# A gated recurrence with a convolution feed-forward on one core: state and head products of a tile's first chunk joined, the last convolution tap joined to the value product, a shorter gate chain, a new order of all steps

## The chip, the cores and the metric

One core of a Trainium2 chip. The time is the device time of one execution in microseconds, median over runs; lower is better.

## What is computed

For each of 4 batches and 8 heads (768 steps, head size 40) a recurrence runs over time, and its gated output (320 features a token) goes through a gated feed-forward. Cut to what matters:

```python
# per step t, for each batch and head
m_new = max(f_gate[t] + m, i_gate[t])
f_stab = exp(f_gate[t] + m - m_new);  i_stab = exp(i_gate[t] - m_new);  m = m_new
C = f_stab * C + i_stab * outer(v[t], k[t]);   n = f_stab * n + i_stab * k[t]
y[t] = sigmoid(o_gate[t]) * (C @ q[t]) / max(abs(n @ q[t]), 1)
# x = y with heads side by side: (4, 768, 320)
gate = sigmoid(sum_k conv_w[k] * x[t - 4 + k])        # 5 taps, per feature
out  = (gate * (x @ w_val)) @ w_out
```

## The kernel before

The recurrence is computed in chunks of 64 steps. Time is cut into 6 tiles of 128 tokens (`j`), each tile into two chunks (`p` = 0, 1), and for each tile and batch (`b`) there is a unit `u = 4j + b` and a group `g = 2u + p`: 48 groups of 8 heads. For one group:

- `args` (L582) makes the exponents of the decay matrix by one matmul from two packed tables, `la` and `ra`, that come from the gates; `expo` (L586) is their exponential on ScalarE, `scores` (L599) the products of q and k (fp16 pieces), `probs` (L604) their product on VectorE, into `pk[:, h, 0:64]`.
- `keyw` (L612, VectorE or GpSimd) puts the weighted unit keys beside it, into `pk[:, h, 64:104]`.
- `heads` (L639) multiplies `pk[:, h, 0:64]` (64 columns of weights) with the values and the incoming state `vc`: 8 products in float32, each of which the engine runs as two records, 16 in all. The first chunk's output stands in partitions 0 to 63 of a bank, the second's in 64 to 127 of the same bank. `state` (L622) multiplies `pk[:, h, 64:104]` (40 columns) with the same values, 16 records into another bank, and `stout` (L631) copies the new state out.

`norm` (L654, L656, L658: three small VectorE operations on the bank), `rsm` (L662) and `gate` (L665) finish a unit of x. `xtr` (L687) transposes x; `xhc`, `xcc`, `x3c`, `xlo`, `xeh`, `xel` split it into a rounded float32r part and a rest. Features 0 to 255 are convolved on GpSimd and VectorE (`cv0` L723, `cv` L729). The last 64 features stand twice, as high and low part, in the 128 partitions of `x3`, and are convolved on TensorE: `cv3` (L750), 5 taps with diagonal weights `cdh` and 5 with `cdl`. `g3c` copies that out, `sigm` (L761) is the sigmoid, `val` (L771) the value product, for three blocks of columns (`m` = 0, 1 with 128 columns, `m` = 2 with 64), 8 matmuls each; `zmul`, `zhi`, `zlo` and `outp` (L794, 8 matmuls per batch) make the output. The inputs of a tile are scaled, cut into fp16 pieces (`hi` L540, `lo` L549) and transposed by TensorE (`trp`, first tiles) or DMA (`trd`, L561).

At the start the gates go through a chain, `gates` (steps 0 to 11, once for tile 0 and once for the rest): a scan for the running maximum, differences, a clamp, a running sum, and a split into three bf16 pieces (`gsp`), which DMAs carry through DRAM into `la` and `ra`.

Nothing is scheduled at run time. `PLAN` is a string of steps with their arguments, `=V`, `=A`, `=P`, `=S` naming the engine or queue, `#n` the PSUM bank (8 banks); steps are issued in that order, so each engine's queue is its own part of the string. All engines wait for each other by semaphores where data or buffers ask for it; two `pk` and three `dm` buffers alternate over the groups.

Of the kernel before, what the change touches and what calls it, by code (L numbers as in the profile page):

```python
# [24 lines left out]
ldc.3=S zrst0.1=V scs.0.0.2.0.1.1=V gates.0.6=V hi.0.0.0=A hi.0.0.1=P raj.4=V ldc.2=S ldq.1.3=S mx.0.3.1=A ovc.0.0=P
scs.0.0.2.0.1.3=V gates.0.3=P gates.1.4=V ldo.1=S raj.2=A fsel.1=P mx.0.2.1=A ldk.1.2.4=S gates.0.7=V fsel.2=P
idk0.2=V gates.0.8=A raj.3=P raj.5=A cpk.0.1.0=V ovc.0.1=P zvc.0=V ctl=P wcv.5.5=A mx.0.2.0=A mx.1.3.0=A lo.0.0.0=V
gates.1.5=P mx.0.3.0=A scs.0.0.2.2.3.0=V idk1.1=A lo.0.0.1=V ovc.1.0=P wcv.5.0=V gates.0.9=V ftl.1=P scs.0.0.2.1.2.0=V
gates.0.10=V scs.0.0.2.1.2.1=V scs.0.0.2.3.4.0=V gates.0.11=P hi.0.1.1=A id16c=P soa.0.2=S hi.0.1.0=P soa.0.1=A
trp.0.0.1#0 lo.0.1.1=V trp.0.0.0#1 ldk.1.0.2=S idk1.0=A lo.0.1.0=V soa.0.3=S mx.1.1.0=A raj.1=V trp.0.1.0#2  # L30
scs.0.0.2.3.4.1=V trc.0.0.1=V hi.0.3.0=V ldo.0=S wcv.5.1=V lo.0.3.0=V wld.0.0=S sigo.1=A gates.1.3=V trp.0.3.0#3
zcmp.1.0=V wcv.5.2=V laj=V mx.1.3.1=A trp.0.1.1#4 scs.0.0.2.2.3.1=V scs.0.0.2.0.1.2=V scs.0.0.2.1.2.2=V hi.0.2.1=A
gates.1.6=V mx.1.1.1=A hi.0.3.1=A raj.0=V soa.0.0=S wcv.5.3=V sog.0=A gates.1.7=V mx.1.2.1=A cla.1=S wcv.5.4=V
gates.1.8=V mx.1.2.0=A hi.0.2.0=V gates.1.9=P trc.0.0.0=A trc.0.1.0=V trc.0.1.1=V mx.1.0.1=A lo.0.2.0=V mx.1.0.0=A
scores.3#5 sia.0.0=S sig_.0=S lo.0.3.1=V sigo.0=A trp.0.2.0#6 scs.1.0.1.0.4.0=V zxc=V wcv.0.0=V lo.0.2.1=V sia.0.1=S
trc.0.3.0=A scs.1.1.2.0.4.0=V cpk.0.0.1=S trp.0.3.1#7 scs.0.0.2.3.4.2=V wcv.0.1=V ldv.0.0=S scs.0.0.2.2.3.3=V
scores.1#0 scs.0.0.2.1.2.3=V scs.0.0.2.3.4.3=V zcmp.1.1=V ldq.2.1=S wcv.0.2=V gates.1.10=V scores.0#2
scs.1.0.1.0.4.1=V wcv.0.3=V args.0#1 trp.0.2.1#4 selg=V expo.0=A ldv.0.1=S wcv.5.6=V wcv.0.4=V args.3#3 trc.0.2.0=A
scs.1.1.2.0.4.1=V zcmp.0.0=V scores.2#1 trc.0.2.1=V cpk.0.1.1=S hi.1.1.1=P sct0=V hi.1.0.0=A scores.4#4 keyw.0=V
probs.0=V args.1#6 hi.1.1.0=A lo.1.0.0=V heads.0#2 expo.1=A lo.1.1.0=V ldk.2.0.2=S trc.0.3.1=A state.0#6 probs.1=V  # L40
ldq.2.3=S expo.3=A keyw.1=V scores.5#0 gates.1.11=V trp.1.0.0#7 stout.0=A args.2#3 chh=A scs.0.0.2.2.3.2=V args.4#6
cdd.0.1=P expo.2=A heads.1#2 ldq.2.2=S soa.1.3=A probs.2=V state.1#3 ldq.2.0=S scs.1.1.2.0.4.2=V heads.2#1 chl=V
wld.1.1=S norm.0.0=V stout.1=A probs.3=V cdd.1.3=P zx3=P wcv.0.5=A soa.1.1=S keyw.2=V hi.1.2.0=A trp.1.1.0#3
norm.0.1=V sog.1=S norm.0.2=V state.2#5 expo.4=A rsm.0=V soa.1.2=S hi.1.0.1=A probs.4=V args.5#6 keyw.4=P soa.1.0=S
expo.5=A wcv.0.6=V heads.4#4 hi.1.3.0=P wld.1.0=S trc.1.0.0=V stout.2=A mx.2.2.0=A cla.0=S open_late=X keyw.3=V
args.6#6 ovc.1.1=P lo.1.3.0=V heads.3#1 mx.2.1.0=A lo.1.2.0=V mx.2.3.0=A state.4#5 smul.1=V gate.0=V trc.1.1.0=A
state.3#7 lo.1.0.1=V probs.5=V sia.1.1=S whi.0.0=A trp.1.2.0#2 wld.2.1=S expo.6=A stout.3=V wlo.0.0=P trp.1.0.1#3
mx.2.0.0=A lo.1.1.1=V sig_.1=S keyw.5=P hi.1.2.1=A trc.1.2.0=V trp.1.1.1#0 wld.2.0=S mx.2.0.1=A scores.7#6 keyw.6=V
xeh.0=P hi.1.3.1=V sout.1#7 trp.1.3.0#2 stout.4=A xel.0=P wcv.1.0=V sia.1.0=S state.5#5 norm.1.0=V trc.1.3.0=A
scs.2.0.1.0.4.0=V trc.1.0.1=V ldk.2.2.4=S heads.5#4 wcv.1.1=V ldv.1.0=S wcv.1.5=A sctc.1=A scs.1.1.2.0.4.3=V args.7#3  # L50
norm.1.1=V lo.1.3.1=V scores.6#2 expo.7=A norm.1.2=V wcv.1.2=V state.6#7 mx.2.1.1=A probs.6=V keyw.7=P cpk.1.0.0=S
args.8#3 norm.2.0=V stout.6=A lo.1.2.1=V rsm.1=P scores.8#2 expo.8=A probs.7=V args.10#7 heads.6#3 zstk.0=P gate.1=V
cdd.1.4=P cpk.1.1.0=S zstk.1=P scs.2.0.1.0.4.1=V wcv.1.3=V mx.2.2.1=A ldq.3.3=S xtr.0#6 probs.8=V hi.2.0.0=A wcv.1.4=P
ldq.3.2=S state.7#1 smul.2=V xhc.0=A hi.2.1.0=P ldv.1.1=S lo.2.0.0=V heads.7#3 mx.2.3.1=A ldq.3.0=S expo.10=A
norm.2.1=V args.9#2 stout.7=V scores.9#7 xeh.1=V expo.9=A keyw.8=P stout.5=V args.11#1 trc.1.1.1=A norm.3.0=V
wcv.2.0=V trp.1.2.1#5 wcv.1.6=V state.8#2 norm.3.1=V xcc.0=A norm.2.2=V xel.1=V expo.11=A scs.2.1.2.0.4.0=V rsm.2=P
scs.2.1.2.0.4.1=V trp.1.3.1#0 ldq.3.1=S stout.8=A lo.2.1.0=V keyw.10=P xtr.1#1 cpk.1.0.1=S x3c.0=A sout.2#2 hi.2.1.1=A
sctc.2=V probs.9=V scores.10#6 trd.2.0.0=S hi.2.0.1=P args.13#2 trc.1.2.1=A gate.2=V heads.8#7 keyw.9=V ldk.3.0.2=S
lo.2.1.1=V state.10#4 xeh.2=V lo.2.0.1=V scores.11#5 stout.10=A xhc.1=V norm.3.2=V wcv.2.5=A heads.9#7 wcv.2.1=V
trd.2.0.1=S rsm.3=P trc.1.3.1=A probs.10=V state.9#4 cdd.1.0=P probs.11=V xcc.1=A heads.10#6 mx.3.2.0=A gate.3=V  # L60
hi.2.2.0=P trd.2.1.0=S mx.3.0.0=A whi.1.0=V heads.11#6 mx.3.3.0=A norm.4.0=V wcv.2.2=V keyw.11=V x3c.1=A cpk.1.1.1=S
expo.13=A args.12#0 norm.5.0=V args.14#5 xeh.3=V lo.2.2.0=V expo.12=A ldv.2.0=S scores.13#3 xel.3=P wcv.2.3=V
mx.3.1.0=A xtr.3#1 ldv.2.1=S norm.5.1=V cdd.0.0=A norm.5.2=V state.11#2 wlo.1.0=V expo.14=A rsm.5=P probs.13=V
hi.2.3.0=A scores.12#0 keyw.12=P gate.5=V xcc.3=A trd.2.1.1=S probs.12=V cdd.0.4=A xlo.0=P state.12#5 stout.11=A
# [867 lines left out]
```

## Time and profile before

| what | us |
|---|---|
| median of 3 runs (259.67 to 263.06) | 260.73 |
| the profiled execution, its own time | 261.67 |
| its span, first to last instruction | 259.8 |
| outside the span | 1.9 |

The durations below come from the profiled execution. The engines run beside each other, so their busy times do not add up to the span; which engine's work stands on the chain that ends last is shown by the chain of waits.

### The profile page before, as it was taken

Reading aid. Unit: us, or ns where it says so; the run is one execution under the profiler, and the core shown is the slowest. Engines: PE = TensorE matmul, PEld = TensorE weight load, DVE = VectorE, ACT = ScalarE, POOL = GpSimd, SP = SyncE. Lnnn points to the kernel's source line nnn. Section 1 sums busy time; section 2 is a strip of 40 time slices with the busy share of each in tenths; the row PEclk is TensorE's granted clock in tenths of the full one; section 3 lists DMA queues with packets and bytes.
Section 4 is the critical chain, followed back from the end, with each engine's and each line's share of the span. In section 5 each row is a group of like instructions: output and inputs, shape, how many; then the busy total and the mean of one; then the engine's idle time right before and its main releaser. Section 6 shows DMA issues by size and latency. Waiting matters only on the chain.

```text
span 259.8 us, 6790 instructions
## 1 busy us (share of the span) xinstructions
PE 218.0 (84%) x2539; PEld 184.8 (71%) x2539; DVE 220.1 (85%) x547; ACT 174.1 (67%) x381; POOL 107.1 (41%) x171
## 2 busy tenths in 40 slices
...
PEclk9999995569999959999999999999999999999999
DMA  8999699799669999979999999699860313001122
GB/s 132 176 169 185 151 144 202 162 174 187 124 96 154 195 209 212 204 116 185 192 159 178 183 193 162 108 176 201 143 112 0 48 46 95 1 28 50 50 103 101
DMA packets 130231, 35.77 MB, mean 138 GB/s; under 512 B 118310, under 2 KB 128086, under 8 KB 130198
## 3 DMA queue, kind: packets, MB, share of 16 engines
...
q8 instruction: 20, 0.33, 0.5%
q10 hardware_dynamic: 560, 0.16, 0.3%
q14 instruction: 13, 0.11, 0.1%
...
## 4 chain that ended last, share of the span: by engine, by line
PE 47%; DVE 22%; DMA 11%; ACT 6%; SPq 6%; issue 5%; POOL 1%; ACTq 0%; DVEq 0%; POOLq 0%
PE bank L639 12%; PE bank L794 8%; PE bank L771 7%; PE bank L622 6%; DVE sg L729 4%; DVE stk L549 4%; DMA tq<-stk 4%; DMA nat<-in_q_dram 4%; PE bank L599 4%; PE bank L582 3%; PE bank L750 3%; PE bank L566 3%; DMA nat<-in_k_dram 2%; PE bank L687 2%; DVE pk L604 2%
## 5 line engine op out<-in xcount | busy, mean ns | idle before, releaser
L639 PEld LDWEIGHTS bank<-vc,pk 104*64 104x64 f32 (+1 forms) x768 | 52.0, 149 | 11.5 <-issue 3.3
L639 PE MATMUL bank<-vc,pk 104*64 104x41 f32 (+1 forms) x768 | 57.1, 241 | 2.6 <-DVE stk L549 1.8
L604 DVE SCALAR_TENSOR_TENSOR pk<-bank,cmp,dm 128x512 f32<-128x512 f32 x48 | 35.5, 743 | 9.3 <-PE bank L599 3.1
L586 ACT ACTIVATE dm<-bank 128x512 f32<-128x512 f32 x48 | 28.4, 600 | 14.7 <-PE bank L582 12.2
L622 PE MATMUL bank<-vc,pk 128*40 128x41 f32 (+1 forms) x704 | 37.2, 212 | 0.9 <-ACT vc L631 0.5
L729 DVE SCALAR_TENSOR_TENSOR sg<-xc,cwt,sg 128x512 f32<-128x512 f32 (+1 forms) x56 | 37.3, 687 | 0.2
L599 PE MATMUL bank<-tq,tk 120*128 120x64 f16 x384 | 27.7, 241 | 11.0 <-DVE tk L570 5.9
L622 PEld LDWEIGHTS bank<-vc,pk 128*40 128x40 f32 (+1 forms) x704 | 32.5, 126 | 3.8 <-issue 2.1
L599 PEld LDWEIGHTS <-tk 120*128 120x128 f16 x384 | 22.5, 119 | 16.4 <-issue 6.7
L540 ACT ACTIVATE stk<-nat,scl 128x640 f16<-128x640 f32 x33 | 27.3, 829 | 6.3 <-PE bank L566 2.9
L566 PE MATMUL bank<-idh,stk 128*120 128x128 f16 x128 | 13.9, 287 | 20.5 <-POOL idh L342 19.1
L549 DVE SCALAR_TENSOR_TENSOR stk<-nat,scl,stk 128x320 f16<-128x320 f32 x48 | 27.4, 578 | 4.2 <-ACT stk L540 2.6
L612 POOL TENSOR_TENSOR pk<-kp,dm 104x320 f32<-104x320 f32 (+1 forms) x23 | 18.9, 827 | 28.8 <-ACT dm L586 12.5
L566 PEld LDWEIGHTS <-stk 128*120 128x120 f16 x128 | 12.7, 193 | 21.2 <-POOL vc L375 17.7
L494 ACT ACTIVATE junk<-nat 128x320 bf16<-128x320 f32 x48 | 22.5, 468 | 7.7 <-DMA nat<-in_k_dram 4.6
L631 ACT COPY vc<-bank 40x328 f32<-40x328 f32 x36 | 15.4, 426 | 16.1 <-PE bank L622 15.7
L662 POOL TENSOR_TENSOR rs<-sg,den 128x320 f32<-128x320 f32 x14 | 11.6, 831 | 28.7 <-DVE den L658 28.6
L582 PE MATMUL bank<-ra,la 120*128 120x512 bf16 x48 | 19.1, 424 | 1.7 <-ACT dm L586 1.6
L794 PE MATMUL bank<-woh,zh 128*128 128x320 f32 x72 | 19.6, 328 | 0.0
L794 PE MATMUL bank<-wol,zh 128*128 128x320 f32 x72 | 18.5, 310 | 0.0
L723 POOL TENSOR_SCALAR sg<-xc,cwt 128x512 f32<-128x512 f32 (+1 forms) x14 | 10.4, 746 | 13.0 <-DVE zl L786 11.1
L544 POOL TENSOR_SCALAR stk<-nat,scl 128x640 f16<-128x640 f32 x10 | 9.1, 912 | 15.5 <-DVE ob L798 6.6
...
## 6 DMA issues: line engine op xcount, KB each, us to landing
...
```

What stands on the lines that cost most here:

```text
L494: A.activation(junk, part(j, x, i), AF.Abs, accum_out=amx[j % 2][:, x, i : i + 1])
L540: A.activation(o, s, AF.Copy, scale=f)
L549: V.scalar_tensor_tensor(t[:, :, c : c + D], part(j, x, i), scl[j % 2][:, x, i : i + 1], t[:, :, 0:D], op0=ALU.mult, op1=ALU.subtract,)
L566: nc.tensor.transpose(t[0:K3, h], stk[(j * B + i) % NSTK][:, x, h, 0:K3], id16)
L582: nc.tensor.matmul(psd, la[:, p, j, b], ra[:, :, j], start=True, stop=True)
L586: A.activation(dms[g % NDM], late["psd", g], AF.Exp)
L599: nc.tensor.matmul(o, tk[h], tq[:, h], start=True, stop=True)
L604: V.scalar_tensor_tensor(pks[g % NPK][:, :, 0:L], late["pss", g], cmp_[j % 2][:, p, b : b + 1], dms[g % NDM], op0=ALU.mult, op1=ALU.mult,)
L622: nc.tensor.matmul(pc[n0 : n0 + D, h], pks[g % NPK][0:n, h, L:], vc[j % 2][0:n, p, b * H + h], start=True, stop=True)
L639: nc.tensor.matmul(ph[p * L : (p + 1) * L, h], pks[g % NPK][0:n, h, 0:L], vc[j % 2][0:n, p, b * H + h], start=True, stop=True,)
L729: V.scalar_tensor_tensor(o, xc[j % 2][:, c, b0:b1, t : t + P], cwt[:, c, t : t + 1], o, op0=ALU.mult, op1=ALU.add)
L794: nc.tensor.matmul(po, z, w, start=(i == 0), stop=(i == len(mm) - 1))
```

## The change

- `both` replaces `heads` and `state` of every first chunk (24 of the 48 groups): one product with all 104 columns of `pk[:, h]`, heads in partitions 0 to 63 and state in 64 to 103 of one bank. It needs `probs` and `keyw`.
- `cv3` and `val` of block `m = 2` share a bank. `w_val`'s weight tiles get 384 columns; columns 256 to 319 hold the diagonal of the fifth tap for the last 64 features (zeros for the others, `zcd`), columns 320 to 383 the last 64 columns of `w_val`. `cv3` is now two matmuls with 128 columns of weights (fifth tap and value product of the last features at once) and 8 with 64 columns for the other taps; `val` for `m = 2` adds 6 matmuls to the same bank. `zmul` reads partitions 64 to 127 of it.
- The gate chain loses a step (4): i minus maximum is no longer formed, the sum is built from `f + m_prev - i` clamped on both sides, and the tile `res` goes.
- `norm`'s first step may run on ScalarE as an absolute value; 14 of 24 do.
- `PLAN` is written anew as a whole: order, engines and banks of all steps. Counts of steps by engine that differ most: `xlo` on GpSimd 11 to 18 (VectorE 13 to 6), `keyw` on GpSimd 23 to 27 (VectorE 21 to 17), `hi` on ScalarE 33 to 27 (VectorE 5 to 11), `gates` on GpSimd 4 to 1 (VectorE 18 to 20). First chunks with `keyw` on GpSimd: 10 to 14 of 24.

```diff
-zero.oh=P zkp=P ldf=A ldi=S zero.tr=V zero.io=V ldk.0.1.2=S zcmp.0.1=V zero.id=V zero.tl=V zrst.1=P ldq.0.0=S
+zero.oh=P zstk.0=P zcmp.0.1=P ldf=A ldi=S zero.tl=V ldq.0.0=S zero.sel=V fsel.0=P fsel.1=P ldq.0.1=S zero.id=P
...
-    cdh = cst.tile([P, 5, L], F32R, name="cdh")
-    cdl = cst.tile([P, 5, L], F32R, name="cdl")
-    wvh, wvl, woh, wol = (cst.tile([P, 3, DM], F32R, name=n) for n in ("wvh", "wvl", "woh", "wol"))
+    cdt = cst.tile([P, 8, L], F32R, name="cdt")
+    wvh, wvl = wvs = [cst.tile([P, 3, 3 * P], F32R, name=n) for n in ("wvh", "wvl")]
+    woh, wol = (cst.tile([P, 3, DM], F32R, name=n) for n in ("woh", "wol"))
...
         elif s == 3:
-            E.tensor_sub(ig[:, cs], ig[:, cs], mg[:, cs])
-        elif s == 4:
-            E.tensor_sub(fg[:, f0:c1], fg[:, f0:c1], mg[:, f0:c1])
+            E.tensor_sub(fg[:, f0:c1], fg[:, f0:c1], ig[:, f0:c1])
         elif s == 5:
-            E.tensor_scalar_max(fg[:, cs], fg[:, cs], GMIN)
+            E.tensor_scalar(ig[:, cs], fg[:, cs], 0.0, GMIN, op0=ALU.min, op1=ALU.max)
...
         elif s == 7:
-            E.tensor_sub(ga[BH:, cs], ig[:, cs], ga[0:BH, cs])
+            V.scalar_tensor_tensor(ga[BH:, cs], fg[:, cs], 0.0, ga[0:BH, cs], op0=ALU.max, op1=ALU.add)
...
-        if s == 0:
+        if s == 0 and e == "A":
+            A.activation(d, nq, AF.Abs)
+            late["na", u] = True
+        elif s == 0:
             V.tensor_scalar(d, nq, -1.0, sct[j % 2][:, b : b + 1], op0=ALU.mult, op1=ALU.max)
+        elif s == 1 and ("na", u) in late:
+            V.tensor_scalar_max(d, d, sct[j % 2][:, b : b + 1])
...
-        mm = [(w[:, t], xe[:, b0:b1, t : t + P]) for w in (cdh, cdl) for t in range(5)]
-        for i, (w, x) in enumerate(mm):
-            nc.tensor.matmul(pg[0:L], w, x, start=(i == 0), stop=(i == len(mm) - 1))
+        for i, w in enumerate(wvs):
+            nc.tensor.matmul(pg, w[:, 2, 2 * P :], xe[:, b0:b1, 4:], start=(i == 0), stop=False)
+        for i in range(8):
+            nc.tensor.matmul(pg[0:L], cdt[:, i], xe[:, b0:b1, i % 4 : i % 4 + P], start=False, stop=False)
...
-        mm += [(w[:, 2, ms], xe[:, b0:b1, 4:]) for w in (wvh, wvl)]
+        if m < 2:
+            mm += [(w[:, 2, ms], xe[:, b0:b1, 4:]) for w in (wvh, wvl)]
         for i, (w, x) in enumerate(mm):
-            nc.tensor.matmul(pf[0:n], w, x, start=(i == 0), stop=(i == len(mm) - 1))
+            nc.tensor.matmul(pf, w, x, start=(m < 2 and i == 0), stop=(i == len(mm) - 1))
```

`both` stands in the kernel before as well, unused there:

```python
    def both(b_, g):
        u, p, j, b = ujb(g)
        ph = late["ph", u] = late["pc", g] = bank(b_, H, DT)
        for h in range(H):
            nc.tensor.matmul(ph[0 : L + D, h], pks[g % NPK][:, h], vc[j % 2][:, p, b * H + h], start=True, stop=True)
```

VectorE's queue at the start, before (`mg`, `fg`, `ig` are the gate tiles, 32 rows; 32x128 is tile 0, 32x640 the rest; L440 the scan of the maximum, L444, L448 and L450 the steps 2, 4 and 5):

```order
L440 SCALAR_TENSOR_TENSOR mg<-fg,ig 32x128
L444 TENSOR_TENSOR fg<-fg,mg 32x127
L382 TENSOR_REDUCE sel_b<-ident 128x4
L369 COPY kp<-ident 40x1280
L442 MEMSET fg 32x1
L448 TENSOR_TENSOR fg<-fg,mg 32x127
L440 SCALAR_TENSOR_TENSOR mg<-fg,mg,ig 32x640
L358 CAST tk_97<-iota_s 128x64
L444 TENSOR_TENSOR fg<-fg,mg 32x640
L312 MEMSET rst 32x2
L450 TENSOR_SCALAR fg<-fg 32x128
```

and after the change (there L436, L440, L442 and L444 are the scan and the steps 2, 3 and 5):

```order
L436 SCALAR_TENSOR_TENSOR mg<-fg,ig 32x128
L440 TENSOR_TENSOR fg<-fg,mg 32x127
L338 CAST idh<-ident 128x128
L436 SCALAR_TENSOR_TENSOR mg<-fg,mg,ig 32x640
L438 MEMSET fg 32x1
L300 MEMSET iota_s 128x64
L371 MEMSET vc_82 64x32
L440 TENSOR_TENSOR fg<-fg,mg 32x640
L308 MEMSET rst 32x2
L442 TENSOR_TENSOR fg<-fg,ig 32x127
L381 TENSOR_REDUCE sel_g<-ident 128x32
L444 TENSOR_SCALAR ig<-fg 32x128
```

The scan now stands behind a copy that waits for GpSimd's selects (three rows ahead of this piece), the 40-row copy and the 128x4 sum are gone from between, and step 4 has no counterpart.

TensorE's queue in the middle of the program, around the value product of tile 1's last block of columns, before (`vc` with `pk` are head and state products, 64x41 and 40x41; `xh`, `xl`, `x` with `wvh`, `wvl` value products; a row with x8 is 16 records):

```order
L582 MATMUL bank_70<-ra,la 128x512
L639 MATMUL bank_72<-vc_82,pk_120 64x41 x8
L622 MATMUL bank_70<-vc_82,pk_120 40x41 x8
L771 MATMUL bank_73<-xh_622,wvh 64x512 x2
L771 MATMUL bank_73<-xh_622,wvl 64x512 x2
L771 MATMUL bank_73<-xl_624,wvh 64x512 x2
L771 MATMUL bank_73<-x_89,wvh 64x512
L771 MATMUL bank_73<-x_89,wvl 64x512
L771 MATMUL bank_69<-xh_622,wvh 128x512 x2
L771 MATMUL bank_69<-xh_622,wvl 128x512 x2
L771 MATMUL bank_69<-xl_624,wvh 128x512 x2
L771 MATMUL bank_69<-x_89,wvh 128x512
```

and after, around the convolution of tile 1 (L748 and L750 are `cv3`, L642 `both`, L616 `state`, L633 `heads`, L771 `val`):

```order
L642 MATMUL bank_73<-vc_81,pk_118 104x41 x8
L616 MATMUL bank_72<-vc_81,pk_119 40x41 x8
L633 MATMUL bank_73<-vc_81,pk_119 64x41 x8
L522 LDWEIGHTS spg
L522 MATMUL bank_74<-sel_b,spg 128x4
L748 MATMUL bank_68<-x_89,wvh 128x512
L748 MATMUL bank_68<-x_89,wvl 128x512
L750 MATMUL bank_68<-x_89,cdt 64x512 x8
L771 MATMUL bank_72<-xh_674,wvh 128x512 x2
L771 MATMUL bank_72<-xh_674,wvl 128x512 x2
L771 MATMUL bank_72<-xl_676,wvh 128x512 x2
L771 MATMUL bank_72<-x_88,wvh 128x512
```

The 64-column value matmuls with `x` are gone: the two 128-column rows of `cv3` stand for them and for the fifth tap. A first chunk is one row of 104 columns.

## Rows read from the trace of the kernel before

**Rows 1.** The head of the profile's page: busy time and share of the span for each engine (PE = TensorE's matrix products, PEld its weight loads, DVE = VectorE, ACT = ScalarE, POOL = GpSimd), then some of the 40 equal slices of the span (6.5 us each; a digit is a busy share in tenths, PEclk the granted TensorE clock in tenths of full speed).

```profile
span 259.8 us, 6790 instructions
PE 218.0 (84%) x2539; PEld 184.8 (71%) x2539; DVE 220.1 (85%) x547; ACT 174.1 (67%) x381; POOL 107.1 (41%) x171
...
PEclk9999995569999959999999999999999999999999
DMA  8999699799669999979999999699860313001122
```

**Rows 2.** The chain of work that ended last, as shares of the span by engine.

```profile
PE 47%; DVE 22%; DMA 11%; ACT 6%; SPq 6%; issue 5%; POOL 1%; ACTq 0%; DVEq 0%; POOLq 0%
```

**Rows 3.** The span in stretches of 13 us: the stretch, its length, then busy us and number of instructions for PE, PEld, DVE, ACT and POOL, the granted TensorE clock, the busy share of the DMA engines, GB/s.

```profile
13.00:26.00 13.00, 4.76 (x40) 4.52 (x40) 10.15 (x30) 10.95 (x27) 6.26 (x11) 1.00 1.18 177
26.00:39.00 13.00, 6.18 (x89) 5.39 (x90) 12.79 (x39) 11.62 (x20) 2.43 (x2) 1.00 0.89 147
39.00:52.00 13.00, 13.00 (x136) 10.88 (x132) 8.37 (x21) 7.16 (x17) 2.37 (x6) 0.54 0.86 182
52.00:65.00 13.00, 12.21 (x187) 11.02 (x185) 10.05 (x25) 8.86 (x22) 5.56 (x11) 0.81 1.15 181
...
91.00:104.00 13.00, 13.00 (x158) 10.62 (x157) 10.66 (x30) 8.25 (x18) 2.42 (x5) 0.74 1.25 211
...
234.00:247.00 13.00, 13.00 (x88) 11.74 (x87) 11.63 (x27) 5.67 (x16) 3.85 (x8) 1.00 0.16 50
...
sum 259.80, PE 218.00 PEld 184.78 DVE 220.13 ACT 174.06 POOL 107.13; mean PE 10.90 PEld 9.24 DVE 11.01 ACT 8.70 POOL 5.36
```

**Rows 4.** The last chain in order of time: start in us, length in us, engine, the bank that is written, line, how many instructions are merged. L639 are head products, L622 state products, L771 value products, L687 transposes, L750 the convolution by matmul, L794 the output product.

```profile
84.03 4.92 DMA tq<-stk
...
158.78 1.06 PE bank L639 x16
...
168.44 0.74 PE bank L622 x16
...
186.93 3.73 PE bank L771 x16
...
215.29 0.88 PE bank L639 x13
...
216.33 0.42 PE bank L622 x11
216.75 0.76 PE bank L639 x13
...
224.75 3.71 PE bank L794 x24
...
236.36 0.33 PE bank L687 x3
...
239.81 1.19 PE bank L750 x10
```

**Rows 5.** Groups of instructions by line and tile over the whole span: line, engine, operation, out<-in, shapes, count, then busy us, mean ns of one, idle time before.

```profile
L639 PEld LDWEIGHTS bank<-vc,pk 104*64 104x64 f32 (+1 forms) x768 | 52.0, 149 | 11.5 <-issue 3.3 <-DVE pk L604 2.6 <-DVE stk L549 2.0
...
L622 PEld LDWEIGHTS bank<-vc,pk 128*40 128x40 f32 (+1 forms) x704 | 32.5, 126 | 3.8 <-issue 2.1 <-ACT ob L798 0.4 <-ACT dm L586 0.4
...
L612 POOL TENSOR_TENSOR pk<-kp,dm 104x320 f32<-104x320 f32 (+1 forms) x23 | 18.9, 827 | 28.8 <-ACT dm L586 12.5 <-PE bank L622 11.4 <-ACT vc L631 4.9
...
L612 DVE TENSOR_TENSOR pk<-kp,dm 128x320 f32<-128x320 f32 (+1 forms) x21 | 10.8, 513 | 2.0 <-PE bank L622 0.9 <-ACT dm L586 0.7 <-issue 0.4
...
L712 POOL TENSOR_TENSOR xl<-xc,xh 128x256 fp32r<-128x256 f32 x11 | 8.7, 796 | 0.6 <-ACT xc L704 0.6
...
L712 DVE TENSOR_TENSOR xl<-xc,xh 128x256 fp32r<-128x256 f32 x13 | 6.3, 500 | 0.0
...
L654 DVE TENSOR_SCALAR den<-bank,sct 128x8 f32<-128x8 f32 x24 | 5.2, 216 | 1.3 <-PE bank L639 1.2
...
L542 DVE TENSOR_SCALAR stk<-nat,scl 128x640 f16<-128x640 f32 x5 | 2.7, 538 | 0.7 <-PE bank L566 0.7
...
L450 POOL TENSOR_SCALAR fg<-fg 32x640 f32<-32x640 f32 x1 | 1.9, 1933 | 0.1
...
L448 DVE TENSOR_TENSOR fg<-fg,mg 32x127 f32<-32x127 f32 (+1 forms) x2 | 1.6, 814 | 0.0
```

**Rows 6.** The timeline of the start (all engines): start us, length us, engine, line, operation, out<-in, shapes, and in brackets the idle time before it with what ended it.

```profile
3.77 0.63 DVE L440 TENSOR_TENSOR_SCAN mg<-fg,ig 32x128 f32<-32x128 f32 x1 [1.66 <-DMA fg<-in_f_gate_dram]
...
4.44 0.28 DVE L444 TENSOR_TENSOR fg<-fg,mg 32x127 f32<-32x127 f32 x1
...
8.50 1.19 POOL L372 MEMSET vc<- 64x1312 f32 x1
...
8.65 1.11 DVE L450 TENSOR_SCALAR fg<-fg 32x128 f32<-32x128 f32 x1
...
18.39 0.42 POOL L463 TENSOR_TENSOR gsp<-res,gsp 64x128 bf16<-64x128 f32 x1 [0.23 <-DVE scl L510]
...
19.10 2.81 PE L566 MATMUL bank<-idh,stk 128*120 128x128 f16 x24 [19.10 <-POOL idh L342]
...
33.39 0.60 ACT L586 ACTIVATE dm<-bank 128x512 f32<-128x512 f32 x1 [0.63 <-PE bank L582]
...
38.06 0.92 PE L639 MATMUL bank<-vc,pk 128*64 128x41 f32 x13 [1.76 <-DVE stk L549]
```

More of the change, by code (lines that the diff above doesn't have):

```diff
@@ L25 @@
[L25 to L64, printed above, removed]
@@ new lines @@
+lo.2.2.0=V expo.16=A whi.2.2=P state.13#7 cv.0.0.2.0.4=V expo.15=A both.14#3 cdd.1.4=P norm.6.0=A norm.4.1=V
+norm.5.2=V trd.2.2.0=S wcv.3.0=V keyw.15=P probs.15=V args.20#6 keyw.16=P stout.14=V sigo.1=A ldv.2.0=S whi.2.3=V
+heads.15#3 cv0.0.1.0.4=P norm.4.2=V ldv.2.1=S hi.2.2.1=A state.15#5 rsm.5=V rsm.4=V stout.13=A cpk.2.1.0=S lo.2.2.1=V
+norm.7.0=A args.18#7 gate.4=V stout.15=V scores.17#1 xeh.4=P xlo.3=P gate.5=V scores.16#5 expo.17=A norm.7.1=V
+cdd.1.1=P norm.7.2=V args.19#4 whi.2.1=A scores.19#2 probs.16=V wlo.2.2=P trd.2.2.1=S xeh.5=A norm.6.1=V rsm.7=V
```

298 lines of the change are left out of this document (171 added, 127 removed).

## The prediction

> **What bounds the kernel now.** First the head of the page [rows 1]: PE is busy for 218.0 of 259.8 us and DVE for 220.1, ACT for 174.1, POOL for 107.1. Two engines are near full, so neither alone says what a change is worth. The chain that ended last [rows 2] has PE for 47% of the span and DVE for 22%, DMA for 11%. The table by stage [rows 3] then shows where: up to 39 us PE has done 4.76 and 6.18 us of work in two stretches and nothing before 19.10 us [rows 6]; from there to the end it is busy for 218.0 - 4.76 - 6.18 = 207.1 of 220.8 us, or 94%. So there are two regimes. The start waits for data, gates and VectorE; the first exponential runs at 33.39 us and the first head product at 38.06 [rows 6]. After that the kernel is a TensorE queue with few gaps, into which VectorE, nearly as full, feeds the factors; the reader sees it in the end of the chain, where one product follows on another [rows 4].
>
> Two stretches of that queue run slowly. The granted clock is 0.54 from 39 to 52 us, 0.81 in the next stretch and 0.74 from 91 to 104 us [rows 3], that is, 1.2 instead of 2.4 GHz for part of them. Ahead of the first, TensorE was busy for 6.18 of 13 us; ahead of the second the chain stands for 4.92 us on a transposing DMA [rows 4].
>
> **Heads and state of a first chunk in one product.** Sixteen head records (64 columns of weights) take 1.06 us, sixteen state records (40 columns) 0.74 [rows 4]. The difference is 0.32 us for 16 x 24 columns, 0.83 ns a column, and the weight loads differ alike (149 and 126 ns, [rows 5]). By that slope 104 columns take 1.06 + 16 x 40 x 0.00083 = 1.59 us. Apart, the pair costs 1.80 us, so joining saves 0.21. But where the two follow on each other, into different halves of the partitions, they partly run together: the heads begin at 215.29, and the next heads after their state at 216.75 [rows 4], 1.46 us for the pair, and there joining costs 0.13. I take half of the 24 pairs for each case: 12 x 0.13 - 12 x 0.21 = -1.0 us. Bounds: if columns cost nothing, the joined product takes 1.06 and 24 x 0.74 = 17.8 us are saved; if each record takes what a transpose with 128 columns takes, 0.33 / 3 = 0.11 us [rows 4], it is 16 x 0.11 = 1.76 against 1.46, and 24 x 0.30 = 7.2 us are lost. I stay by the slope, since it comes from the same instruction.
>
> **The last tap in the value product.** For the last block of columns 8 matmuls become 6. Seven such blocks (five of 512 moving columns, two of 256) lose 10 of the long and 4 of the short kind. A long one takes 3.73 / 16 = 0.233 us, a short one 1.19 / 10 = 0.119 [rows 4]: 2.33 + 0.48 = 2.8 us. `cv3` keeps ten matmuls; that two of them have 128 columns instead of 64 costs nothing, as the 0.233 us is that of 128 columns already. A new wait comes with it: the copy of the convolution to `sg` (and the sigmoid behind it on ScalarE) now stands behind 6 more matmuls on the same bank, 6 x 0.233 = 1.4 us, seven times. Bounds: 0 to 9.8 us. I take 0: the order puts those 6 close behind `cv3`, and TensorE has other products to run.
>
> TensorE is thus relieved of 3.8 us. Since it is busy for 94% of the time from 39 us on, I count 0.8 of that: -0.8 for the first part, -2.2 for the second.
>
> **VectorE.** Off it go 7 `xlo` at 500 ns, 4 `keyw` at 513 and 14 first steps of `norm` at 216 [rows 5], 3.5 + 2.1 + 3.0 = 8.6 us, and step 4 of the gates with 1.6. On to it come 6 `hi` at 538 ns, 3.2 us, and a 640-column gate step from GpSimd, 0.8 by the mean of step 4. That is -6.2, and I say -6, since some twenty smaller moves go either way. VectorE has 22% of the chain where TensorE has 47%; I count a third, -2.0 us (bounds 0 and -6). What takes it over: GpSimd gets 7 x 0.796 + 4 x 0.827 = 8.9 us and loses its 1.93 us gate step [rows 5], 7.0 more on an engine busy for 41%; ScalarE gets 14 small absolute values, which no row shows. Their cost is between nothing and the 0.60 us of a 128x512 exponential [rows 6]; near the 0.2 us that VectorE takes for the same shape, 2.8 us, against 6 `hi` that leave it. Both have idle time, so I cost them at nothing; if that cover fails, the reciprocal, `rsm` and `gate` of a unit come later.
>
> **The start.** The gate chain runs from 3.77 us to the last bf16 piece at 18.39 + 0.42 on POOL [rows 6]. Step 4 is gone from it, and GpSimd has three of its steps fewer, so that there are fewer changes of engine. Against that, the first scan now stands behind the copy of the selects, which waits for GpSimd; I see it 1 to 2 us later than 3.77. The chain behind it is some 3 us shorter. Net -1.5 us, bounds 0 and -3. The DMAs are the same in number and size, and SP's queue takes over two gate transfers that ScalarE issued; I cost that at nothing while the first products wait for VectorE anyway.
>
> **The sum.** -0.8 - 2.2 - 2.0 - 1.5 = -6.5 us. The profiled execution took 261.67 us, so 255.2. The median of the runs shown is 260.73, 0.94 lower; the forecast is 254.2 us.
>
> **Rivals.**
> *No change: VectorE's relief comes back.* A 32x128 VectorE step took 1.11 us beside a GpSimd memset of 1.19 us that began just before it; another 32-row step of that width took 0.28 [rows 6]. So the two can hold each other up. If all of the 7.0 us that GpSimd gains are lost on VectorE, it gains 1 us instead of losing 6, +0.3 on the chain; with the start unchanged and the TensorE terms at a half instead of 0.8 (-1.9), the sum is -1.6: about 259.1. For it: with 11.01 of 13 us on the mean [rows 3], VectorE has little idle time to lose it in. Against it: many of GpSimd's steps overlap with VectorE work that reads PSUM. The Trainium skill, SBUF — State Buffer (Who interferes with whom), says that a VectorE instruction with two SBUF inputs and a reading GpSimd instruction exclude each other for a whole instruction. `xlo` and `keyw` are such on GpSimd. The slow step above fits the same section's other case, a VectorE operation in a two-port mode against any operation of GpSimd: 1.11 us is about its own 0.28 and most of the 1.19 beside it.
>
> *Slower: the first chunk gets longer.* If the joined record goes at 0.11 us, 7.2 us are lost; and the heads now wait for `keyw` too, which GpSimd makes in 14 of the 24 first chunks, 0.31 us later than VectorE would: 4.4 us. With the other terms, +7.2 + 4.4 - 2.2 - 2.0 - 1.5 = +5.9: 266.6 us. It decides where a record takes over about 0.1 us and TensorE has nothing queued ahead that hides `keyw`. For it: the overlapped pair of 1.46 us. Against it: the slope, and several TensorE steps between a chunk's exponents and its product. The Trainium skill, TensorEngine Tiling (Key Properties), has it that different tiles of the array load weights and multiply in parallel. By that a pair would cost only its longer half, 1.06 us, and joining would lose 0.53 us each, 12.7 in all, and the time would come out at about 268. The trace bears that out for a part: 1.46 of 1.80 us, an overlap of some records, not of a whole product.
>
> *More than forecast: a slow stretch goes.* At 0.74 of the clock the stretch from 91 us loses 0.26 x 13 = 3.4 us. If the new order keeps TensorE fed through the wait of 4.92 us ahead of it, this comes back, with some of the wait: -6.5 - 3.4 - 1.3 = -11.2, or 249.5 us. Against it: the same transposes stand in the new order.
>
> **Chances.** The forecast 0.48, with a range of its own from 251 to 258.5; no change 0.21; slower 0.14; a slow stretch gone 0.17. A measurement of this kernel can tell about 2%, 255.5 us and 265.9. Of the forecast's share 0.31 lies below 255.5 and 0.17 above; with 0.17 from the last rival, faster has 0.48. Same has 0.17 + 0.21 and 0.01 of the slower case, 0.39; slower 0.13. The range from 248 to 262 leaves out the slower case and a little at the low end; the dear end of the joined product lies beyond it.
>
> **What would show it.** In the profile after: head and state records of first chunks gone, 384 records of `both` at about 92 ns from start to start (right between 85 and 98; 110 is the slower rival); 14 value matmuls fewer; VectorE's sum of busy times lower by 4 to 8 us and POOL's higher by 5 to 10; the first exponential at 31 to 33 us; TensorE still over 90% busy behind the start. I am wrong if TensorE gains idle time in the middle, if `xlo` and its VectorE neighbours grow by a third, or if the slow clock stretches differ from two.

## The result and the profile after

The changed kernel takes 250.0 us (median of 4 runs, 249.65 to 252.14) beside 260.39 for the kernel before on the same chip: ratio 0.960, with a 95% interval of 0.951 to 0.969. In a later set of runs it took 250.74 beside 258.60: 0.968 (0.965 to 0.972). The gain is 8 to 10 us; the forecast of 254.2 said 6.5.

One thing about the profiled executions first. Where the granted clock is recorded, that of before had 23.9 us at 1.2 GHz and took 261.67 us, that of after 6.8 us and 249.69. Among 43 later runs of the kernel before, the six whose granted clock was below 0.955 took 260.9 to 263.2 us (mean 262.3), the twenty at 0.975 or more 256.6 to 260.5 (mean 258.3). So some 4 of the 12 us between the two profiles go with the clock of that one execution. The ratios leave out a kernel's executions that took over 1.5% more than its fastest.

The head of the page after, answering to [rows 1]:

```profile
span 247.9 us, 5992 instructions
...
PE 210.1 (85%) x2141; PEld 180.4 (73%) x2141; DVE 221.7 (89%) x523; ACT 171.3 (69%) x395; POOL 119.6 (48%) x187
...
PEclk9999999979999799999999999999999999999999
```

VectorE is busy for 221.7 us, as long as before (220.1), though work was meant to leave it; its idle time fell from 39.7 to 26.2 us. The 11.9 us between the spans are these 13.5 us less the 1.6 us of added work. The chain of waits, for [rows 2], has TensorE no longer far ahead:

```profile
PE 29%; DVE 26%; DMA 14%; ACT 10%; issue 8%; POOL 7%; SPq 3%; ACTq 0%; POOLq 0%; DVEq 0%
```

Where the idle time went shows in stretches of 65 us (busy us and count of PE, PEld, DVE, ACT, POOL, then granted clock, DMA share, GB/s). Before:

```profile
0.00:65.00 65.00, 36.15 (x441) 31.80 (x441) 51.10 (x137) 45.37 (x98) 26.99 (x53) 0.87 1.01 168
65.00:130.00 65.00, 58.47 (x821) 48.56 (x816) 59.38 (x151) 52.17 (x119) 33.27 (x45) 0.95 1.09 169
130.00:195.00 65.00, 63.64 (x758) 52.24 (x755) 57.25 (x143) 47.30 (x105) 26.14 (x39) 1.00 1.00 161
195.00:259.80 64.80, 59.74 (x533) 52.17 (x532) 52.41 (x119) 29.21 (x61) 20.72 (x37) 1.00 0.18 52
```

After:

```profile
0.00:65.00 65.00, 38.15 (x438) 33.30 (x439) 57.67 (x155) 51.63 (x117) 26.63 (x53) 0.97 0.96 162
65.00:130.00 65.00, 59.78 (x670) 49.76 (x668) 59.89 (x140) 53.06 (x126) 39.63 (x57) 0.97 1.20 169
130.00:195.00 65.00, 62.66 (x645) 52.89 (x645) 60.43 (x136) 43.03 (x95) 36.49 (x52) 1.00 1.06 170
195.00:247.90 52.90, 49.49 (x395) 44.43 (x395) 43.73 (x95) 23.58 (x58) 16.82 (x26) 1.00 0.19 59
```

By 65 us VectorE has done 57.67 us of work where it had done 51.10: 6.6 of the 13.5 us of idle time are saved there, 0.5 in the next stretch, 3.2 between 130 and 195 us and 3.2 at the end.

The start, for [rows 6]. SP's queue before (DMA issues: a weight load `raw`, the gates' pieces `gda`, the tables `la` and `ra`, the values `vc`):

```profile
22.06 3.74 SPq L816 DMA_DIRECT2D raw<-in_moe_w_val_dram  x1
25.84 0.70 SPq L472 DMA_DIRECT2D gda<-gsp  x1
28.82 0.34 SPq L483 DMA_DIRECT2D la<-gda  x1
29.27 1.03 SPq L479 DMA_DIRECT2D ra<-gdg  x1
31.54 0.68 SPq L424 DMA_DIRECT2D vc<-in_v_dram  x1
```

and after, with the first exponential, the first `probs` (L598) and the first joined product (L642):

```profile
19.88 1.47 SPq L466 DMA_DIRECT2D gda<-gsp  x2
23.65 1.05 SPq L477 DMA_DIRECT2D la<-gda  x1
24.80 0.84 SPq L473 DMA_DIRECT2D ra<-gdg  x1
26.29 0.67 SPq L420 DMA_DIRECT2D vc<-in_v_dram  x1
31.53 0.60 ACT L580 ACTIVATE dm<-bank 128x512 f32<-128x512 f32 x1
32.32 0.75 DVE L598 SCALAR_TENSOR_TENSOR pk<-bank,cmp,dm 128x512 f32<-128x512 f32 x1
33.19 2.95 PE L642 MATMUL bank<-vc,pk 128*104 128x41 f32 x16
```

The tables and the values are issued some 5 us earlier, and the first product starts at 33.19 instead of 38.06. The gates are not what the old order waits for here: tile 0's last piece was made by 18.81 us [rows 6], but the last transfers of its pieces were issued at 25.14 us by ScalarE's queue and at 25.84 by SP's, there behind the weight load that holds the queue for 3.74 us. In the new order the last two are issued from 19.88 us on.

Pieces of the last chain, for [rows 4] (L642 a joined product, L771 the 6 value matmuls of the last columns):

```profile
179.96 1.59 PE bank L642 x16
...
220.33 1.39 PE bank L771 x6
```

and groups, for [rows 5] (L606 is VectorE's `keyw`, L711 `xlo`, L653 the second step of `norm` behind ScalarE's first, L728 the convolution on VectorE):

```profile
L728 DVE SCALAR_TENSOR_TENSOR sg<-xc,cwt,sg 128x512 f32<-128x512 f32 (+1 forms) x56 | 40.2, 732 | 0.2
L642 PEld LDWEIGHTS bank<-vc,pk 128*104 128x104 f32 x384 | 38.8, 178 | 3.8 <-DVE pk L606 1.1 <-issue 0.7 <-ACT den L648 0.5
...
L711 POOL TENSOR_TENSOR xl<-xc,xh 128x256 fp32r<-128x256 f32 x18 | 15.3, 853 | 8.5 <-ACT xh L699 6.3 <-ACT xc L703 1.8 <-DVE xc L703 0.3
L653 DVE TENSOR_SCALAR den<-den,sct 128x8 f32<-128x8 f32 x14 | 3.9, 276 | 0.7 <-ACT den L648 0.7
```

### The profile page after: what moved, and what is told of

Read it like the earlier page. It is cut to its first block, busy times and chain, and to the rows that moved or that the text cites. A ratio compares the mean times of both kernels' runs of the same rounds, so it can differ in the third digit from the quotient of the medians.

```text
span 247.9 us, 5992 instructions
## 1 busy us (share of the span) xinstructions
PE 210.1 (85%) x2141; PEld 180.4 (73%) x2141; DVE 221.7 (89%) x523; ACT 171.3 (69%) x395; POOL 119.6 (48%) x187
## 4 chain that ended last, share of the span: by engine, by line
PE 29%; DVE 26%; DMA 14%; ACT 10%; issue 8%; POOL 7%; SPq 3%; ACTq 0%; POOLq 0%; DVEq 0%
PE bank L642 7%; DMA sg<-in_o_gate_dram 5%; PE bank L633 5%; DVE sg L728 4%; PE bank L793 4%; DVE stk L543 3%; PE bank L771 3%; DMA out_dram<-ob 3%; ACT sg L761 2%; ACT junk L488 2%; DMA tq<-stk 2%; DVE pk L598 2%; DVE sg L776 2%; PE bank L593 2%; PE bank L560 2%
## 5 line engine op out<-in xcount | busy, mean ns | idle before, releaser
L642 PE MATMUL bank<-vc,pk 128*104 128x41 f32 x384 | 41.3, 270 | 1.7 <-DVE pk L606 1.0
L642 PEld LDWEIGHTS bank<-vc,pk 128*104 128x104 f32 x384 | 38.8, 178 | 3.8 <-DVE pk L606 1.1
L728 DVE SCALAR_TENSOR_TENSOR sg<-xc,cwt,sg 128x512 f32<-128x512 f32 (+1 forms) x56 | 40.2, 732 | 0.2
L598 DVE SCALAR_TENSOR_TENSOR pk<-bank,cmp,dm 128x512 f32<-128x512 f32 x48 | 35.4, 740 | 3.3 <-PE bank L593 2.4
L606 POOL TENSOR_TENSOR pk<-kp,dm 128x320 f32<-128x320 f32 (+1 forms) x27 | 22.8, 849 | 21.5 <-ACT dm L580 9.1
L560 PE MATMUL bank<-idh,stk 128*120 128x128 f16 x128 | 13.7, 280 | 21.1 <-DVE stk L543 20.8
L633 PEld LDWEIGHTS bank<-vc,pk 104*64 104x64 f32 x384 | 24.6, 140 | 8.7 <-issue 2.7
L633 PE MATMUL bank<-vc,pk 104*64 104x41 f32 x384 | 27.4, 233 | 3.2 <-ACT vc L625 1.3
L543 DVE SCALAR_TENSOR_TENSOR stk<-nat,scl,stk 128x320 f16<-128x320 f32 x48 | 28.8, 605 | 1.5 <-POOL stk L538 1.3
L560 PEld LDWEIGHTS <-stk 128*120 128x120 f16 x128 | 12.5, 187 | 23.1 <-DVE stk L543 22.1
L534 ACT ACTIVATE stk<-nat,scl 128x640 f16<-128x640 f32 x27 | 21.8, 827 | 8.2 <-DVE scl L504 3.7
L661 POOL TENSOR_TENSOR rs<-sg,den 128x320 f32<-128x320 f32 x16 | 12.6, 788 | 29.6 <-DVE den L657 29.5
L711 POOL TENSOR_TENSOR xl<-xc,xh 128x256 fp32r<-128x256 f32 x18 | 15.3, 853 | 8.5 <-ACT xh L699 6.3
```

The source lines that it names most:

```text
L534: A.activation(o, s, AF.Copy, scale=f)
L543: V.scalar_tensor_tensor(t[:, :, c : c + D], part(j, x, i), scl[j % 2][:, x, i : i + 1], t[:, :, 0:D], op0=ALU.mult, op1=ALU.subtract,)
L560: nc.tensor.transpose(t[0:K3, h], stk[(j * B + i) % NSTK][:, x, h, 0:K3], id16)
L598: V.scalar_tensor_tensor(pks[g % NPK][:, :, 0:L], late["pss", g], cmp_[j % 2][:, p, b : b + 1], dms[g % NDM], op0=ALU.mult, op1=ALU.mult,)
L606: eng[e].tensor_mul(pks[g % NPK][0:n, :, L:], kp[0:n, p, b * H : (b + 1) * H], dms[g % NDM][0:n, :, L - 1 : L].to_broadcast([n, H, D]),)
L633: nc.tensor.matmul(ph[p * L : (p + 1) * L, h], pks[g % NPK][0:n, h, 0:L], vc[j % 2][0:n, p, b * H + h], start=True, stop=True,)
```

## Experiments

Two theories stood at the beginning: the removed work makes the gain, as the forecast's sum has it; or the new order makes it. Within the second: the slow clock, the start, or the packing as a whole.

### The new order with the old arithmetic

```diff
         for h in range(H):
-            nc.tensor.matmul(ph[0 : L + D, h], pks[g % NPK][:, h], vc[j % 2][:, p, b * H + h], start=True, stop=True)
+            nc.tensor.matmul(ph[0:L, h], pks[g % NPK][:, h, 0:L], vc[j % 2][:, p, b * H + h], start=True, stop=True)
+        for h in range(H):
+            nc.tensor.matmul(
+                ph[L : L + D, h], pks[g % NPK][:, h, L:], vc[j % 2][:, p, b * H + h], start=True, stop=True
+            )
...
-norm.u.0=A
+norm.u.0=V
```

Beside these, two matmuls with zero weights stand in each `val` of the last columns, and the old gate chain.

> The new order with the old arithmetic: in the kernel after the change, every joined product of a first chunk is again 8 head and 8 state products (one bank), the value product of the last columns has its two extra matmuls back (zero weights), the gate chain has its step 4 back, and the first step of norm is on VectorE. Theory A, the order brings most of the gain, because the long stretch at 1.2 GHz is gone: 252 to 254 us, with at most 10 us at half clock where the kernel before has 23.9. Theory B, the removed work brings it: 258 to 261 us.

Measured: 248.83 us, ratio 0.958 (0.952 to 0.965). The new list, that is, the order with its engines and banks, makes all of the gain that can be measured; the four edits of the arithmetic add nothing to it. They are not all that the forecast priced at -6.5 us: the moves of `xlo`, `keyw` and `hi` between engines, most of its term for VectorE, are part of the list and stand here as after the change. The last experiment takes them back. Its first stretch of 65 us, and the head of its page:

```profile
0.00:65.00 65.00, 35.67 (x521) 30.34 (x521) 57.76 (x160) 51.86 (x115) 27.40 (x53) 0.97 0.94 159
...
span 247.2 us, 6785 instructions
...
PE 207.1 (84%) x2539; PEld 176.4 (71%) x2539; DVE 220.0 (89%) x539; ACT 170.2 (69%) x381; POOL 121.3 (49%) x187
```

VectorE has done 57.76 us here, as after the change, and over the span it is busy for 220.0 of 247.2 us, idle for 27.2. TensorE's busy time fell too, from 218.0 to 207.1 us for the same 2539 records. Where it is recorded, the clock makes at most 8.6 us of that (half of 23.9 less 6.8 us). So that the order acts through VectorE's idle time is a reading of this account; no run separates it from TensorE's.

### The short gate chain in the old order

```diff
-gates.0.3=P gates.0.4=V
+gates.0.3=V
-gates.1.3=V gates.1.4=V
+gates.1.3=V
```

> The old order with the short gate chain alone: step 4 is gone, the rest of the old list is as it was. By the forecast's term for the start, -1.5 us: about 259 us, first head product at 36 to 37 us instead of 38.06. If the start is worth what the new kernel shows (first product at 33.2 us) and the gate chain makes it: 255 to 257. If the chain isn't what the first product waits for: 260.4, no change.

Measured: 0.996 (0.991 to 1.000), no change within 2%; the median of all 10 runs is 259.04 us. TensorE's first head product of this run, in the timeline with what it waited for:

```profile
38.31 1.58 PE L680 MATMUL bank<-vc,pk 128*64 128x41 f32 x13 [2.34 <-DMA vc<-in_v_dram]
```

The first product waits for the load of the values, not for the gates: as before, the load's issue stands in SP's queue behind the tables, and these behind the weight load.

### Joining in the old order

```diff
-heads.g#a ... state.g#b        (g = 0, 2, ..., 21 of 24 groups)
+both.g#a
```

> The old order with 21 of the 24 first chunks joined (heads and state in one product of 104 columns; banks reassigned where the longer use asks for it; the three other groups stay apart). By the forecast, 21/24 of -0.8: 259.7 us. If the joined product or its wait for keyw is dear, as in the slower rival (7.2 + 4.4 us): 265 to 272. If the joining brings most of the gain: 252 to 255.

Measured: 280.33 us, 1.082 (1.073 to 1.090). It is no measure of the joining: in 12 of the 21 groups the joined product stands ahead of that group's `probs` in the list, so it multiplies older factors, and `probs` waits for it. The list does show why the old order could not take the change: in 15 of the 24 first chunks `state` stands ahead of `probs`, in 19 ahead of `heads`, and a joined product gives that up.

### Warming TensorE before the slow stretch

```diff
 trp.0.1.0#2
+warm.10#5
...
 trp.0.1.1#4
+warm.40#5
```

> The old kernel with 50 added transposes of the identity, 10 at 22 us and 40 at 25 us, into a bank not yet in use, where TensorE waits for VectorE (1.2 and 4.7 us idle). Nothing else is changed. Theory A (the long stretch at half clock follows the sparse start): time at 1.2 GHz falls from 23.9 to under 12 us, and the time by half of that, 253 to 256 us. Theory B (the stretch has nothing to do with how busy TensorE was): 259.5 to 261.5, half clock as before. Theory C (activity brings it on): it begins earlier or lasts longer, 261 to 266.

Measured: 261.07 us, 1.009 (1.005 to 1.014): no faster, and no change within 2%. The granted clock of its profile, and the first transposes of tile 0 (L610) beside the added ones (L616):

```profile
PEclk9999779579999659999999999999999999999999
...
18.84 2.80 PE L610 MATMUL bank<-idh,stk 128*120 128x128 f16 x24 [18.84 <-POOL idh L386]
...
23.82 2.40 PE L616 MATMUL bank<-idh 128*128 128x128 f16 x40
```

The added work did bring the fast clock earlier: a transpose takes 117 ns in the first row and 60 in the second. But the clock fell again at 28.8 us, while TensorE was idle for 3.32 us, and the slow stretches are still there, 27.3 us in all, one of them earlier. Filling up the sparse start doesn't pay; what sets the clock is left open.

### Where in the order

Lists that begin in one order and go on in the other, with the old arithmetic. In the three that begin with the old order an absolute value is written in place ahead of other reads of its buffer, so that weights of the convolution (in the third also of a projection) are not the reference's; instructions and shapes are the same.

```diff
-PLAN = new order
+PLAN = first 222 (382, 600) steps of the old order, then the remaining steps in the new one
```

> Old arithmetic throughout (as in a_order); the first 222 steps of the list stand in the order of the kernel before (to the second group's products, some 40 us of its trace), everything behind them in the new order. The gain of the new order was about 10 us. Theory S, the start carries it (first head product 5 us earlier): 257 to 260 us. Theory M, the stretch from 40 to 110 us carries it: 248 to 251. Theory E, it is spread evenly: 250 to 252.

> As h_old_start, with the first 382 steps in the old order (nine groups, some 65 to 75 us of the old trace), the rest in the new one. Theory S: 257 to 260 us. Theory M: 253 to 256. Theory E: 251 to 253. If the old start leaves a debt that the new rest can make good: 248 to 250.

> As h_old_start, with the first 600 steps in the old order (18 groups, some 105 us of the old trace), the rest in the new one. Theory S and theory M: 257 to 260 us, since all that they name is old here. Theory E: 253 to 255. If the tail carries the gain: 248 to 250.

> The other way round: old arithmetic, the first 361 steps in the new order (eight groups, some 58 us of the new trace), the rest in the old order. Theory S: 249 to 252 us. Theory M: 253 to 256. Theory E: 256 to 258.

Measured: 253.43 us, 0.982 (0.973 to 0.991) with the old start; 255.70, 0.988 (0.981 to 0.995) with 382 old steps; 259.17 (254.96 to 262.55) beside 258.62 with 600, too scattered for a ratio; 266.30, 1.029 (1.023 to 1.035) with the new start and the old rest. The kernel with all of the new order, 248.83 us, was measured on another chip. So when the first 40 us are put back, they cost 4.6 of the 10 us by the medians, 6.2 by the ratios, and 1.4 to 2.3 more by 65 us, a step that is within the two intervals. In VectorE's first stretch with the old start

```profile
0.00:65.00 65.00, 34.66 (x454) 30.08 (x455) 52.19 (x147) 47.79 (x108) 29.50 (x55) 0.92 0.98 161
```

there are 52.19 us of work instead of 57.76; the 5.6 us are never made up. The opposite list is no gain at all. Its stretch ahead of the seam, one behind it, and in that the longest waits of ScalarE and VectorE (L715 the sigmoid `sigo`, L647 `probs`):

```profile
0.00:52.00 52.00, 26.02 (x363) 22.16 (x364) 47.05 (x123) 40.49 (x90) 24.52 (x46) 0.90 0.87 157
...
52.00:78.00 26.00, 16.16 (x224) 13.75 (x221) 13.52 (x41) 17.13 (x30) 9.13 (x16) 0.74 1.04 140
...
64.03 1.27 ACT L715 ACTIVATE sg<-sg 128x1280 f32<-128x1280 f32 x1 [4.81 <-DMA sg<-in_o_gate_dram]
...
67.24 0.75 DVE L647 SCALAR_TENSOR_TENSOR pk<-bank,cmp,dm 128x512 f32<-128x512 f32 x1 [7.89 <-ACT dm L629]
```

Up to 52 us VectorE did 47.05 us of work, nearly as much as in the new order (47.69) and 6.0 more than before (41.05). Behind the seam it works for 13.52 us of 26. There the old rest first issues what the new start had put off, and the load of the output gates stands right ahead of the sigmoid that reads it: ScalarE waits for the load, and VectorE 7.89 us for the exponential behind the sigmoid. So this list loses its lead at its own seam, and does not tell what the new start is worth in front of the old rest. The seams of these lists have a cost of their own, so the differences are sizes, not shares.

### Only the first product earlier

```diff
-selg=V ... wcv.5.6=V wcv.0.4=V ... sct0=V ... keyw.0=V probs.0=V ... heads.0#2 ... probs.1=V
+keyw.0=V probs.0=V heads.0#2 ... probs.1=V selg=V wcv.5.6=V wcv.0.4=V sct0=V
```

> The kernel before with eight steps of its list moved: keyw, probs and heads of group 0 stand ahead of four small VectorE steps that group 0 doesn't need (sel_g, two weight conversions, the copy to sct) and of a copy for tile 0; nothing else. If VectorE's queue holds the first product back, it comes at about 35.4 us instead of 38.06. If the start's gain passes on to the end (the old start cost 4 us in front of the new rest): 256 to 258 us. If the rest of the old order takes it back: 258.5 to 259.5, no change.

Measured: 1.003 (0.998 to 1.008), no gain. That ratio stands on 4 of 12 runs; the median of all 12 is 263.51 us, at granted clocks from 0.929 to 0.980. `probs` (L647) came at 34.58 instead of 36.41, and then, in the timeline of this run,

```profile
34.58 0.74 DVE L647 SCALAR_TENSOR_TENSOR pk<-bank,cmp,dm 128x512 f32<-128x512 f32 x1
...
37.55 1.13 PE L682 MATMUL bank<-vc,pk 128*64 128x41 f32 x16 [2.35 <-DMA vc<-in_v_dram]
```

the product waited 2.35 us for the values. In the old order VectorE's factors and SP's values both come only at 37 to 38 us; an order has to move both to start earlier. No run moved the issue of the values, or of the weight load ahead of it, alone.

### The joined product taken apart, the engines put back

The kernel after the change was measured once more beside two edits of it. The first edit takes the joined products apart, as the first piece of the diff of `a_order`, the new order with the old arithmetic, does; the second:

```diff
-xlo.u=P (7)  keyw.g=P (4)  hi.j.b.x=V (6)  norm.u.0=A (14)
+xlo.u=V      keyw.g=V      hi.j.b.x=A      norm.u.0=V
```

> The kernel after the change once more, beside the next three on the same chip: 0.96 of the kernel before, as measured, 249 to 250 us.

> The kernel after the change with each joined product taken apart again: 8 head products, then 8 state products, same bank, same place. By the forecast's term the joining saves 0.13 to 0.21 us a pair, so this should be 0 to 5 us slower: 250 to 253. If the pairs overlap more than the one pair that the forecast read (1.46 us against 1.59 for the joined product), 24 x 0.13 = 3 us of TensorE time come back: 247 to 249. If the time does not hang on this much TensorE work: within 0.5 us of the kernel after.

> The kernel after the change with the forecast's moves of work off VectorE taken back: 7 xlo and 4 keyw from GpSimd to VectorE, 6 hi from VectorE to ScalarE, the first step of norm on VectorE in all 24 units. Forecast: VectorE has 5.4 us more to do, a third of it shows, +1.8 us, 251 to 252. If VectorE is the bound of the new order: +4 to +6 us, 254 to 256. If the port that VectorE and GpSimd share ate the relief: no change, or 0.5 to 1 us faster, with the conv step of VectorE back from 732 ns towards 690.

Measured: after again 250.74 us, 0.968 (0.965 to 0.972); apart 248.47, 0.961 (0.957 to 0.965); engines put back 249.29, 0.965 (0.961 to 0.969). Taken apart it is 1.8 us faster by the ratios, but the two intervals touch, and its runs had higher granted clocks, 0.978 to 0.998 against 0.944 to 0.977 for after again. The runs nearest in clock took 249.17 and 250.01 us apart (0.978 and 0.979), 248.00 joined (0.977). So the joining shows neither a gain nor a loss. The timeline of after again around a joined product, behind the heads of a second chunk (L633):

```profile
177.16 1.13 PE L633 MATMUL bank<-vc,pk 104*64 104x41 f32 x16 [0.86 <-ACT vc L625]
178.22 1.66 PE L642 MATMUL bank<-vc,pk 128*104 128x41 f32 x16
179.71 0.42 PE L686 MATMUL bank<-ident,x 128*128 128x128 f32 x2
```

and apart (L642 heads, L644 state):

```profile
177.19 0.95 PE L633 MATMUL bank<-vc,pk 104*64 104x41 f32 x13 [1.47 <-ACT vc L625]
177.92 0.25 PE L642 MATMUL bank<-vc,pk 128*64 128x41 f32 x1
177.97 0.23 PE L633 MATMUL bank<-vc,pk 104*64 104x41 f32 x1
...
178.83 0.62 PE L644 MATMUL bank<-vc,pk 128*40 128x41 f32 x12
179.39 0.44 PE L690 MATMUL bank<-ident,x 128*128 128x128 f32 x2
```

From start to start of what follows, heads and joined product take 2.55 us, heads, heads and state 2.20: the 0.35 us go with records that write different halves of the partitions and alternate in the trace. From its own first record to the next instruction the joined product takes 1.49 us (median of 22), the pair 1.44 (median of 14).

With the engines put back, VectorE is busy for 220.8 us, against 220.6 for after again. The heads of the two pages, after again first, and groups of the run with the engines put back:

```profile
PE 208.0 (84%) x2141; PEld 179.3 (73%) x2141; DVE 220.6 (90%) x523; ACT 171.4 (70%) x395; POOL 117.6 (48%) x187
...
PE 209.7 (84%) x2141; PEld 181.3 (73%) x2141; DVE 220.8 (89%) x542; ACT 173.5 (70%) x387; POOL 107.8 (43%) x176
...
L649 DVE TENSOR_TENSOR pk<-kp,dm 128x320 f32<-128x320 f32 (+1 forms) x21 | 10.5, 498 | 2.5 <-DMA kp<-nat 1.5 <-ACT dm L623 0.9
L754 DVE TENSOR_TENSOR xl<-xc,xh 128x256 fp32r<-128x256 f32 x13 | 6.4, 494 | 1.2 <-ACT xc L746 1.2
```

Against after again, `xlo` takes 3.5 us more on VectorE (6.4 and 2.9), `keyw` 1.0 (10.5 and 9.5), `norm`'s first two steps 1.3 (8.9 and 7.6), `hi` 3.3 less (2.7 and 6.0): 2.5 us more by the groups' sums, 0.2 in busy time. Part of the difference is in other groups (`lo` 27.5 and 28.9). Instructions on VectorE also overlap in the trace, where their durations add up to 253.1 and 252.1 us, so that what is taken off in one place need not all be given back. Since VectorE's load stayed the same, the run doesn't tell whether VectorE bounds the new order.

## Why the prediction was right, and where it was wrong

The verdict, faster, is the one with the highest chance. The time, 250.0 us, lies in the stated range from 248 to 262, but 1 us below the likeliest case's own range from 251 to 258.5. The reasons are mostly not those of the sum, so that it came as near as it did is luck in good part.

- **Heads and state in one product** (-0.8 us): the size of a record was right, 92 ns from start to start over 384 records. The step "I take half of the 24 pairs for each case" failed: 1.80 us for a pair apart was two rows added up; the 14 pairs of the new order that run without a wait and with no other record between took 1.40 to 1.47. The joining costs TensorE 0.05 to 0.35 us each time, and no gain in the whole time shows. The Trainium skill, TensorEngine Tiling (Array Packing), section Key Properties, says that different tiles work in parallel; the trace agrees in part, with 2.20 us where the sum of three products alone would be 2.86 [rows 4].
- **The tap in the value product** (-2.2): the count was right, 14 matmuls fewer (L771 154 instead of 168), 1.39 us for the 6 of a block. The effect did not show: with the two matmuls back, and all else of the arithmetic, the ratio was 0.958 after 0.960, and 0.961 with the pairs alone taken apart. The step that failed is "I count 0.8 of that": a TensorE that is busy for 94% still did not pass its relief on to the end. No run puts the two matmuls back alone.
- **VectorE** (-2.0): its busy time was to fall by 4 to 8 us; it rose by 1.6. The `norm` step on ScalarE (0.18 us each) left VectorE a second step of 276 ns where it had been 159 in the old trace, so it took off 0.10 us a unit, not 0.216; the 0.8 us for the gate step from GpSimd was the mean of two widths, of which the wide one took 1.08; the convolution steps went from 687 to 732 ns, and stayed at 741 with the engines put back, so that the moves to GpSimd are not their cause. The Trainium skill, SBUF — State Buffer (Who interferes with whom), has VectorE and GpSimd exclude each other. The runs show `xlo` on GpSimd at 853 and 838 ns in the two traces of after, instead of 796, but at 835 with 7 of them taken back, so these moves don't tell that rule's share. GpSimd rose by 12.5 us, not 5 to 10. The first rival's "VectorE's relief comes back" describes this term rightly, but not through its price.
- **The start** (-1.5): the first exponential came at 31.53 us, inside 31 to 33, and the first product 4.9 us earlier. The gate chain, from which the term was built, did end 2.4 us earlier (at 16.39 instead of 18.81 us), but in the old order its shortening is worth nothing by itself (0.996). The step that failed is "I cost that at nothing while the first products wait for VectorE anyway": they waited for SP's queue as much, as the traces of the two runs in the old order with a shorter gate chain and an earlier `probs` show.
- **The sum.** -6.5 forecast, -8 to -10 measured, and -10 with the joining, the tap, the gate step and the `norm` step taken back. What the forecast left out is the term that is the answer: the order as a whole, priced at nothing but the start. A row of it was there: VectorE is busy for 8.37 of 13 us from 39 to 52 us [rows 3]. But TensorE is busy for all 13.00 us of that stretch at a clock of 0.54, and part of VectorE's waits end with an exponential that waits for TensorE's `args`, so the row alone does not tell which engine starves which. With the old start put back, VectorE did 8.03 us there at a clock of 0.76.
- **The rivals.** "A slow stretch goes" gave 249.5 and is nearest in time. Two stretches at 1.2 GHz remain, 3.4 us each instead of 17.1 and 6.8; both shrank, and the long one, which the rival does not name, by most. But at a like clock the kernel before still takes 258.3, where the new order with the old arithmetic takes 247.3 to 249.0 (granted clocks of 0.965 to 0.993), so the clock is not the main cause. The slower rival did not come: the record took 92 ns, not 110.
- **TensorE** stayed over 90% busy behind the start, 210.1 less 3.7 and 11.2 up to 39 us, or 195.2 of the 208.9 us behind it.

Open: which moves of the order outside the first 65 us bring the remaining 3 us, and what brings on the slow clock.
